# Two opening blocks' input prepared in chunks beside attention's last pair, with one tile that later blocks reuse

## Chip, cores and metric

The kernel runs on one core of a Trainium2 chip. The metric is the device time of one execution in microseconds (us), the median of several runs. The names of the engines are the profile's: PE is TensorE, PEld its weight load, DVE is VectorE, ACT is ScalarE, POOL is GpSimd, and SP is SyncE, whose queue issues most loads and stores.

## What is computed

Attention over 4 x 8 heads with 576 rows of 64 and rotated q and k, then two layers of two matrices each on its 2304 x 512 result. The reference, cut to what matters:

```python
q_rot, k_rot = rotate(q), rotate(k)
scores = scale * np.matmul(q_rot, k_rot.transpose(0, 1, 3, 2))
attn = softmax(scores)
x = np.matmul(attn, v)                      # 4 x 8 x 576 x 64, then 2304 x 512
h = np.maximum(x @ moe_w_in, 0.0)           # 2304 x 2048
x = h * h @ moe_w_out                       # 2304 x 512
h = x @ moe2_w_in
g = np.maximum(h, 0.0) + alpha * np.minimum(h, 0.0)
out = g @ moe2_w_out
```

The weights come as float64. Every product is made with operands split into a high and a low part, in three matmuls (high by high, high by low, low by high).

## The kernel before

*Attention* takes the heads in 16 pairs and each pair in 9 steps, 144 in all. A step makes scores on PE (L201), their maximum on DVE (L204), the exponential on ACT (L205), transposes on PE (L222, L234, L240, L241), which ACT copies to a high part (pth, ptth, L210) and DVE to a low part (ptl, pttl, L211), and the product with v (L267). POOL rotates k and q (L114 to L118) and splits v (vsplit, L127 and L128). The undivided result goes to x1 in DRAM (the names xd and x), the reciprocal sums (L250 to L258) to r1 (rd and r). SP moves the rotated operands to their places (kH, qT, kL, L169).

*The layers* (moe) work on 6 blocks of 384 columns. In layer 0 a block's x is made from three loads: two halves of x1, which are added (L502 or L533), and the reciprocals, by which the sum is multiplied (L503 or L534). ACT takes its high part xh (L509 or L538), DVE the low part xl (L514 or L543). For each of 16 input weights a unit of 12 matmuls makes ph (L552 to L554), ACT its relu g (L592), ACT or POOL its square; for each of 16 output weights a unit splits g into gh (ACT, L483) and gl (DVE, L484) and adds 12 matmuls to py (L570). The first two blocks run together, weight by weight (FIRST = 2): 32 units for the input weights, then 32 for the output weights. The later blocks use weights that lie ready. In layer 1 DVE makes mn (L595) and POOL adds it to g (L596).

*The weights* of layer 0 are converted while the opening blocks run: a load of 512 KB into one of four w64 buffers (L373), two operations on DVE (L382, L383), one more (L388), one on ACT (grow, L392), two on DVE (L397, L398), and the join on ACT (L403) and DVE (L404). The weights of layer 1 are converted beside the later blocks of layer 0, through one buffer (wc), stored to DRAM (wk, L454), and loaded again later (L460).

*What sets the order.* PE's order is written out everywhere. DVE's, ACT's and POOL's are written out from the layers' start on, and in attention a scheduler sets them. The layers' steps before their first unit run from attention's step 144 on (FOLLOW, follow): load_first, join_first, high_first and low_first for the two opening blocks, whole blocks of 4 chunks of 128x384 in two buffers (xr and r), and the first weights. Their space is what attention's pools ald (raw k, q, v), arope, acst, anat and akq leave, which close at step 143. The later blocks' x goes chunk by chunk (load_x, join_x, high_x, low_x) through one buffer of xr and r (pool xt1); each chunk's four steps are put at units by the job table:

```python
job((NF - 16 if before == (0, FIRST - 1) else at_unit[before + (1, 0)]) + 4 * c + 1,
    ((-2, load_x), (0, join_x), (1, high_x), (2, low_x)), layer, b, c)
```

Of the kernel before, what the change touches and what calls it, by code (L numbers as in the profile page):

```python
# [21 lines left out]
P = 128  # L22
# [14 lines left out]
FOLLOW = 0  # L37
# [4 lines left out]
def attention(tc, q, k, v, ident, ident_d, rope_d, xd, rd, follow):  # L42

# [8 lines left out]
    with ExitStack() as at:  # L52
# [30 lines left out]
        raw = {(x, nm): ld.tile([P, 4, 5, D], F32, name=f"{nm}raw{x}") for x in range(2) for nm in "kqv"}  # L83
# [223 lines left out]
        for s in range(len(steps) + LAG + OP + 3 * OPD + 8):  # L307
# [42 lines left out]
HELD0, OUT0, AHEAD = 4, 9, 2  # L350
XT0, CONV0, EVERY0, EVERY1, EVERY2 = 2, -8, 1.8, 1.8, 2.9
# [57 lines left out]
def moe(tc, xd, rd, mats, pbias, dram, al, out):  # L409
# [11 lines left out]
    with ExitStack() as mo:  # L421
        pool = lambda name, bufs, **kw: mo.enter_context(tc.tile_pool(name=name, bufs=bufs, **kw))
        st = pool("st", 1, side="right")
        held0 = pool("held0", HELD0, side="right")
        ps_h = pool("ps_h", 4, side="right", space=PSUM)
        xfirst = mo.enter_context(ExitStack())
        xtmp = mo.enter_context(ExitStack())
        xp = [xfirst.enter_context(tc.tile_pool(name="xp0", bufs=1, side="right"))]
        xp.append(xtmp.enter_context(tc.tile_pool(name="xt0", bufs=XT0, side="right")))
        mo.enter_context(tc.manual_schedule(engines={ET.PE, ET.DVE, ET.Activation, ET.Pool}))  # L430
# [56 lines left out]
        xin = {}  # L487

        def load_first(b):
            cs = slice(b * W, b * W + W)  # L490
            xr = xp[1].tile([P, KC, 2, W], F32, name="xr")
            r = xp[1].tile([P, KC, W], F32, name="r")
            for j in range(2):
                js = slice(64 * j, 64 * j + 64)
                for y in range(2):
                    nc.sync.dma_start(out=xr[js, :, y], in_=xd[j, 64 * y:64 * y + 64, :, cs])
                nc.sync.dma_start(out=r[js], in_=rd[:, j, cs].unsqueeze(0).to_broadcast([D, KC, W]))
            xin[b] = xr, r
# [232 lines left out]
```

## Time and profile before

| | |
|---|---|
| median of 3 runs | 1196.81 us (1196.57 to 1197.05) |
| profiled execution | 1196.49 us |
| its span in the profile | 1194.7 us |
| mean granted clock of PE | 0.978 of full speed |
| busy: PE, DVE, ACT, POOL | 1097.7, 694.4, 567.9, 378.7 us |
| attention's part | up to about 352 us |
| layer 0's part | about 352 to 760 us |

The sum is made against the profiled execution; the span is 1.8 us shorter than its time. Busy shares are means over the whole span, in which the stretches differ: PE is near full in most, and empty for some 17 us where attention ends.

### The profile page before, as it was taken

What the parts mean: (1) busy time and instruction counts of PE and PEld (TensorE: products, weight loads), DVE (VectorE), ACT (ScalarE), POOL (GpSimd) and SP (SyncE); (2) the same over time, 40 slices, a digit from 0 to 9 for tenths busy, and PEclk for the clock granted to TensorE, in tenths of its full rate; (3) what the DMA queues carried; (4) which work ended last, traced back from release to release, by engine and by line L of the source; (5) the groups of instructions that cost most, each with busy time, mean ns of one, the idle gap of its engine ahead of it and who ended that gap; (6) DMA issues with size and microseconds to landing.
All of it is one profiled execution on the core that took longest, in us unless ns stands there. A gap on an engine that the chain in (4) does not pass through costs nothing.

```text
span 1194.7 us, 17840 instructions
## 1 busy us (share of the span) xinstructions
PE 1097.7 (92%) x6480; PEld 1040.0 (87%) x6480; DVE 694.4 (58%) x1214; ACT 567.9 (48%) x1222; POOL 378.7 (32%) x351
## 2 busy tenths in 40 slices
PE   2899999999749979899999999999999999999998
PEld 1789889898639969799899999999898989899896
DVE  2788888888678887856767582223233332323332
ACT  1687887888625554445464553322223232323222
POOL 7956657650032220122122131113040413223140
PEclk9999999999969989999999999999999999999999
DMA  8867677555663442455757647860101001010101
GB/s 227 193 177 176 179 194 182 138 142 133 180 151 110 124 128 86 143 177 172 245 175 228 209 160 229 262 215 8 47 1 36 19 21 33 14 40 7 40 1 26
DMA packets 97174, 150.17 MB, mean 126 GB/s; under 512 B 21440, under 2 KB 66112, under 8 KB 97088
## 3 DMA queue, kind: packets, MB, share of 16 engines
q1 hardware_dynamic: 91472, 138.85, 41.5%
q10 hardware_dynamic: 5360, 10.07, 2.3%
q8 instruction: 51, 0.84, 0.3%
q14 instruction: 35, 0.29, 0.1%
q0 software_dynamic: 256, 0.13, 0.0%
HBM read 84.98 MB, written 35.73 MB: 101 GB/s over the span
## 4 chain that ended last, share of the span: by engine, by line
PE 60%; DVE 17%; DMA 7%; POOL 5%; ACT 5%; issue 3%; SPq 2%; ACTq 0%; POOLq 0%; DVEq 0%
PE py L570 21%; PE ph L553 9%; PE ph L554 9%; PE ph L552 9%; PE acc L267 4%; DMA xr<-x 3%; PE sc L201 3%; DVE w L397 3%; PE ps L222 2%; DVE m L383 2%; DVE w L404 2%; DMA kraw<-in_k_dram 2%; DVE w L398 1%; DVE nat L144 1%; DVE ptl L211 1%
## 5 line engine op out<-in xcount | busy, mean ns | idle before, releaser
L552 PE MATMUL ph<-xh,w 128*128 128x384 f32 x768 | 259.7, 338 | 9.1 <-ACT xh L538 5.5
L553 PE MATMUL ph<-xl,w 128*128 128x384 f32 x768 | 259.5, 338 | 2.7 <-DVE xl L514 2.2
L554 PE MATMUL ph<-xh,w 128*128 128x384 f32 x768 | 258.7, 337 | 0.0
L484 DVE TENSOR_TENSOR gl<-g,gh 128x384 fp32r<-128x384 f32 x192 | 109.0, 568 | 197.0 <-ACT gh L483 196.8
L596 POOL TENSOR_TENSOR g<-g,mn 128x384 f32<-128x384 f32 x96 | 101.8, 1060 | 295.6 <-DVE mn L595 295.6
L592 ACT ACTIVATE g<-ph 128x384 f32<-128x384 f32 x192 | 94.0, 489 | 202.0 <-PE ph L554 194.4
L570 PE MATMUL py<-w,gh 128*128 128x512 f32 x576 | 177.5, 389 | 0.0
L483 ACT ACTIVATE gh<-g 128x384 fp32r<-128x384 f32 x192 | 99.8, 522 | 154.1 <-PE py L570 130.7
L570 PE MATMUL py<-gh,w 128*128 128x384 f32 x640 | 167.8, 338 | 2.8 <-ACT gh L483 2.8
L552 PEld LDWEIGHTS ph<-xh,w 128*128 128x128 f32 x768 | 145.7, 190 | 12.9 <-ACT xh L538 6.4
L553 PEld LDWEIGHTS ph<-xl,w 128*128 128x128 f32 x768 | 145.6, 190 | 4.0 <-DVE xl L514 2.5
L554 PEld LDWEIGHTS ph<-xh,w 128*128 128x128 f32 x768 | 145.9, 190 | 0.0
L595 DVE TENSOR_SCALAR mn<-ph,al 128x384 f32<-128x384 f32 x96 | 59.3, 618 | 138.8 <-ACT g L592 132.1
L570 PEld LDWEIGHTS py<-w,gh 128*128 128x128 f32 x576 | 108.0, 188 | 22.2
L570 PEld LDWEIGHTS py<-gh,w 128*128 128x128 f32 x640 | 117.5, 190 | 3.5 <-ACT gh L483 3.5
L204 DVE TENSOR_REDUCE nm<-sc 128x1 f32<-128x576 f32 x144 | 105.9, 752 | 23.2 <-PE sc L201 21.6
L205 ACT ACTIVATE p<-sc,nm 128x576 f32<-128x576 f32 x144 | 106.4, 740 | 27.1 <-DVE nm L204 20.1
L570 PE MATMUL py<-w,gl 128*128 128x512 f32 x288 | 112.2, 389 | 0.0
L570 PE MATMUL py<-gl,w 128*128 128x384 f32 x320 | 108.5, 339 | 2.1 <-DVE gl L484 1.7
L211 DVE TENSOR_TENSOR ptl<-ps,pth 128x512 fp32r<-128x512 f32 (+1 forms) x160 | 99.9, 632 | 17.6 <-ACT pth L210 15.4
L600 POOL TENSOR_TENSOR g<-g 128x384 f32<-128x384 f32 x48 | 45.7, 953 | 188.1 <-ACT g L592 179.6
L210 ACT ACTIVATE pth<-ps 128x512 fp32r<-128x512 f32 (+1 forms) x160 | 86.9, 554 | 37.6 <-PE ps L222 36.5
(108 smaller groups left out, 1864.9 us busy)
## 6 DMA issues: line engine op xcount, KB each, us to landing
w<-in_moe_w_in_dram SPq DMA_DIRECT2D x32, 512.0 KB
w<-in_moe_w_out_dram SPq DMA_DIRECT2D x32, 512.0 KB
wk<-w SPq DMA_DIRECT2D x32, 512.0 KB
w<-wk SPq DMA_DIRECT2D x32, 512.0 KB
xr<-x SPq DMA_DIRECT2D x56, 192.0 KB
kH<-nat SPq DMA_DIRECT2D x64, 144.0 KB
qT<-nat SPq DMA_DIRECT2D x64, 144.0 KB
kL<-nat SPq DMA_DIRECT2D x64, 144.0 KB
```

What stands on the lines that cost most here:

```text
L204: V.tensor_reduce(out=nm, in_=sc[:, :, 0:SH], axis=AX.XY, op=ALU.max, negate=True)
L205: A.activation(out=Pt[n, i][:, j * S:(j + 1) * S].rearrange("p (a b) -> p a b", a=2), in_=sc[:, :, 0:SH], func=AF.Exp, bias=nm, accum_out= ...
L210: A.activation(out=sl(hi), in_=src, func=AF.Copy)
L211: V.tensor_tensor(out=sl(lo), in0=src, in1=sl(hi).bitcast(F32), op=ALU.subtract)
L483: A.activation(out=hi, in_=g, func=AF.Copy)
L484: V.tensor_tensor(out=lo, in0=g, in1=hi.bitcast(F32), op=ALU.subtract)
L552: T.matmul(ph[:, :W], lhsT=wh[:, cs], rhs=xh, start=(c == 0), stop=False)
L553: T.matmul(ph[:, :W], lhsT=wh[:, cs], rhs=xl, start=False, stop=False)
L554: T.matmul(ph[:, :W], lhsT=wl[:, cs], rhs=xh, start=False, stop=(c == KC - 1))
L570: T.matmul(acc, lhsT=x, rhs=y, start=(s0 and k == 0), stop=(s1 and k == 2))
L592: A.activation(out=g, in_=ph, func=AF.Relu)
L596: G.tensor_tensor(out=g, in0=g, in1=mn, op=ALU.add)
```

## The change

The opening blocks' x is loaded, joined and split chunk by chunk, by the same four functions as for the later blocks. The loads begin 14 steps before attention's end (AHEAD_X = 14, from step 130 on). For this attention's raw k, q, v, rotation and constants close at step 130 (front), except that their last v has a pool of its own (ald1); anat, akq and the scores' PSUM move to a second group (scored), which closes at step 143. The eight chunks follow each other every one and a half steps; the loads of weights 0 to 3 stand between them, while their conversion stays where it was.

The high and low parts of the opening blocks lie in one tile X (xs); later blocks reuse it in slices, and it also holds the conversion buffer of layer 1's weights (Xw[3]) and two output weights of layer 0 (Xw[4], Xw[5]). A second tile XT (xt) has two buffers for raw x and r, for all blocks, where later blocks had one; mn of layer 1 lies in it too. For the opening blocks both additions and the subtraction that makes the low part are on POOL.

```diff
-FOLLOW = 0
+AHEAD_X = 14
...
-        ld = fpool("ald", 1)
+        lds = [fpool("ald0", 1)]
+        cp = fpool("acst", 1)
         rp = fpool("arope", 1)
-        cp = fpool("acst", 1)
-        nat = fpool("anat", 1)
-        kq = fpool("akq", KQB)
-        front.enter_context(tc.manual_schedule(engines={mybir.EngineType.PE}))
-        ps_sc = fpool("ps_sc", NSC, space=PSUM)
+        lds.append(fpool("ald1", 1))
+        scored = at.enter_context(ExitStack())
+        nat = scored.enter_context(tc.tile_pool(name="anat", bufs=1))
+        kq = scored.enter_context(tc.tile_pool(name="akq", bufs=KQB))
+        scored.enter_context(tc.manual_schedule(engines={mybir.EngineType.PE}))
+        ps_sc = scored.enter_context(tc.tile_pool(name="ps_sc", bufs=NSC, side="right", space=PSUM))
...
+            if s == len(steps) - AHEAD_X:
+                front.close()
             if s == len(steps) - 1:
-                front.close()
-            if s >= len(steps) + FOLLOW:
+                scored.close()
+            if s >= len(steps) - AHEAD_X:
                 follow()
...
-HELD0, OUT0, AHEAD = 4, 9, 2
-XT0, CONV0, EVERY0, EVERY1, EVERY2 = 2, -8, 1.8, 1.8, 2.9
+HELD0, OUT0, OUTX, AHEAD = 4, 7, 2, 2
+CONV0, EVERY0, EVERY1, EVERY2 = -8, 1.8, 1.8, 2.9
...
+        X = pool("x", 1, side="right").tile([P, 2, KC, FIRST * W], F32R, name="xs")
+        Xf = X.rearrange("p y c w -> p (y c w)")
+        Xw = [Xf[:, 1024 * k:1024 * k + 1024].rearrange("p (y n) -> p y n", y=2) for k in range(6)]
+
+        XT = pool("xt", 1, side="right").tile([P, 2, 3, W], F32, name="xt")
         st = pool("st", 1, side="right")
...
         def slot(z, i):
+            if z and OUT0 <= i < OUT0 + OUTX:
+                return Xw[4 + i - OUT0]
...
-            return late["wc"].tile([P, 2, 512], F32R, name="w")
+            return Xw[3]
...
-        def load_first(b):
...
-        def join_first(b):
...
-        def high_first(b):
...
-        def low_first(b):
...
+        xin, xbuf = {}, itertools.cycle(range(2))
 
         def load_x(layer, b, c):
             c0 = b * W
-            xr = xp[1].tile([P, 2, W], F32, name="xr")
-            r = None
+            k = next(xbuf)
+            xr, r = XT[:, k, 0:2], XT[:, k, 2]
...
         def high_x(layer, b, c):
-            xh, xl = (xp[0].tile([P, W], F32R, name=nm) for nm in ("xh", "xl"))
+            if first(layer, b):
+                xh, xl = (X[:, y, c, b * W:b * W + W] for y in range(2))
+            else:
+                xh, xl = (Xf[:, (2 * c + y) * W:(2 * c + y) * W + W] for y in range(2))
...
         def low_x(layer, b, c):
             xh, xl = xsp[layer, b][c]
-            V.tensor_tensor(out=xl, in0=xin.pop((layer, b, c))[0][:, 0], in1=xh.bitcast(F32), op=ALU.subtract)
+            E = G if first(layer, b) else V
+            E.tensor_tensor(out=xl, in0=xin.pop((layer, b, c))[0][:, 0], in1=xh.bitcast(F32), op=ALU.subtract)
...
-                    mn = late["tp"].tile([P, W], F32, name="mn")
+                    mn = XT[:, u % 2, 2]
...
         for k in range(2 * FC):
...
+            if k < HELD0:
+                job(CONV0 + 2 * k, conv[0][1:], 0, 0, k)
+                continue
...
-        for b in range(FIRST):
-            for d, stage in ((-9, load_first), (b - 8, join_first), (2 * b - 7, high_first), (2 * b - 6, low_first)):
-                job(d, ((0, stage),), b)
...
+        for e in range(AHEAD_X):
+            for k in range(FIRST * KC):
+                for d, stage in ((0, load_x), (2, join_x), (2, high_x), (2, low_x)):
+                    if 3 * k // 2 + d == e:
+                        stage(0, *divmod(k, KC))
+            if e % 3 == 1 and e // 3 < HELD0:
+                weights.load(st, 0, 0, e // 3)
+            yield
+        late["held0"] = pool("held0", HELD0, side="right")
+        ps_h = pool("ps_h", 4, side="right", space=PSUM)
+        mo.enter_context(tc.manual_schedule(engines={ET.PE, ET.DVE, ET.Activation, ET.Pool}))
...
-            if t == at_unit[0, 0, 1, 0]:
-                xfirst.close()
-                xp[:] = pool("xp1", KC, side="right"), pool("xt1", 1, side="right")
-                late["wc"] = pool("wc", 1, side="right")
```

How this moves instructions: on POOL, behind the last vsplit (vs) of attention, before:

```order
L127 CAST vs<-vraw_111 128x10x64
L128 TENSOR_TENSOR vs<-vraw_111,vs 128x10x64
L503 TENSOR_TENSOR xr<-xr,r 128x4x384
L502 TENSOR_TENSOR xr<-xr 128x4x384
L503 TENSOR_TENSOR xr<-xr,r 128x4x384
L600 TENSOR_TENSOR g<-g 128x384 x16
```

and now (xt is the raw x, xs the high and low parts; three operations for each of eight chunks, of which the first is shown with what precedes it):

```order
L131 CAST vs<-vraw_114 128x10x64
L132 TENSOR_TENSOR vs<-vraw_114,vs 128x10x64
L512 TENSOR_TENSOR xt<-xt 128x384
L513 TENSOR_TENSOR xt<-xt 128x384
L526 TENSOR_TENSOR xs<-xt,xs 128x384
```

Three operations on whole blocks (and an add on DVE) became 24 on chunks, all of them still behind the last vsplit.

On ACT, around attention's last pth and ptth, before (w are operations of weight 0, xh is the first opening block's high part):

```order
L210 ACTIVATE pth<-ps 128x4x128
L210 ACTIVATE ptth<-ps 128x384
L210 ACTIVATE pth<-ps 128x4x128
L392 ACTIVATE w_4646<-w_4646,pbias 128x512
L509 ACTIVATE xh<-xr 128x4x384
L210 ACTIVATE pth<-ps 128x4x64 x2
L210 ACTIVATE ptth<-ps 128x128
L210 ACTIVATE ptth<-ps 64x64 x2
L255 ACTIVATE ri<-ps 9x128
```

and now:

```order
L214 ACTIVATE pth<-ps 128x4x128
L520 ACTIVATE xs<-xt 128x384
L214 ACTIVATE ptth<-ps 128x384
L214 ACTIVATE pth<-ps 128x4x128
L398 ACTIVATE w_4317<-w_4317,pbias 128x512
L520 ACTIVATE xs<-xt 128x384
L214 ACTIVATE pth<-ps 128x4x64 x2
L214 ACTIVATE ptth<-ps 128x128
L214 ACTIVATE ptth<-ps 64x64 x2
L520 ACTIVATE xs<-xt 128x384
```

The single xh ahead of the last pth became the fifth, sixth and seventh xs, and the seventh stands behind attention's ptth; the eighth follows later, ahead of the join of weight 0. The first xs stands further ahead, between two of the last pair's p:

```order
L209 ACTIVATE p,sums<-sc,nm 128x576
L520 ACTIVATE xs<-xt 128x384
L209 ACTIVATE p,sums<-sc,nm 128x576
L214 ACTIVATE pth<-ps 128x4x128
L214 ACTIVATE ptth<-ps 128x512
```

On SP, at block 3's x loads in layer 0 (wk is a store of a converted weight of layer 1, w the load of a raw one), before:

```order
L525 DMA r<-r_65 64x384 x2
L454 DMA wk_0_5_6672<-w 128x1024
L523 DMA xr<-x_64 64x2x384 x2
L373 DMA w_6797<-in_moe_w_in_dram 128x4x256
L454 DMA wk_0_6_6744<-w 128x1024
L525 DMA r<-r_65 64x384 x2
L373 DMA w_6864<-in_moe_w_in_dram 128x4x256
L523 DMA xr<-x_64 64x2x384 x2
L454 DMA wk_0_7_6818<-w 128x1024
L373 DMA w_6912<-in_moe_w_in_dram 128x4x256
L525 DMA r<-r_65 64x384 x2
L454 DMA wk_0_8_6885<-w 128x1024
```

and now:

```order
L504 DMA xt<-r_65 64x384 x4
L461 DMA wk_0_5_6676<-xs 128x1024
L502 DMA xt<-x_64 64x2x384 x2
L379 DMA w_6792<-in_moe_w_in_dram 128x4x256
L461 DMA wk_0_6_6743<-xs 128x1024
L379 DMA w_6856<-in_moe_w_in_dram 128x4x256
L504 DMA xt<-r_65 64x384 x2
L502 DMA xt<-x_64 64x2x384 x2
L461 DMA wk_0_7_6812<-xs 128x1024
L379 DMA w_6901<-in_moe_w_in_dram 128x4x256
```

The third chunk's x is loaded one weight earlier than before, the fourth two weights earlier, where the third's was.

## Rows read from the trace of the kernel before

**Rows 1.** Stretches: length, busy PE, PEld, DVE, ACT, POOL (instructions), PE's clock, DMA share, GB/s.

```profile
290.00:305.00 15.00, 15.00 (x123) 14.83 (x121) 13.09 (x25) 11.67 (x30) 2.08 (x2) 1.00 0.61 154
370.00:400.00 30.00, 29.86 (x172) 29.54 (x171) 25.41 (x42) 17.68 (x34) 6.29 (x6) 1.00 0.40 123
760.00:1195.00 435.00, 429.03 (x2208) 394.76 (x2206) 135.09 (x237) 121.05 (x244) 102.62 (x97) 1.00 0.15 45
```

**Rows 2.** PE's timeline, 317 to 446 us: start, duration, what [idle before <- releaser].

```profile
339.62 0.42 PE L240 MATMUL ps<-ident,p 128*64 128x128 f32 x1 [16.58 <-DVE pttl L211]
...
352.55 0.33 PE L552 MATMUL ph<-xh,w 128*128 128x384 f32 x1
...
358.05 0.61 PE L553 MATMUL ph<-xl,w 128*128 128x384 f32 x1 [2.22 <-DVE xl L514]
...
444.17 0.69 PE L570 MATMUL ph<-gl,w 128*128 128x384 f32 x1 [2.97 <-DVE gl L484]
```

**Rows 3.** The chain of waits, 318 to 357 us: start, duration, what.

```profile
320.25 10.32 DMA xr<-x
...
332.83 3.43 POOL xr L503
...
352.65 0.61 DVE w L397
...
353.75 0.69 DVE w L404
...
356.25 1.75 DVE xl L514
```

**Rows 4.** What waited for what, 515 to 760 us: us in total, times, longest.

```profile
PE ph L552 <- ACT xh L538: 5.5, 3, 2.3
```

**Rows 5.** Busy time by stretch, behind the first two of these waits.

```profile
586.00:592.00 6.00, 5.62 (x22) 5.36 (x23) 5.45 (x11) 4.59 (x9) 0.30 (x1) 0.72 0.54 177
657.00:663.00 6.00, 5.54 (x21) 5.28 (x22) 4.80 (x10) 3.84 (x8) 0.22 (x1) 0.72 0.60 216
```

**Rows 6.** SP's timeline: two x loads of block 3's chunks.

```profile
567.56 1.25 SPq L523 DMA_DIRECT2D xr<-x  x2
...
577.13 1.26 SPq L523 DMA_DIRECT2D xr<-x  x2
```

**Rows 7.** POOL's timeline: the last vsplit, and two adds of block 3.

```profile
303.64 1.54 POOL L128 TENSOR_TENSOR vs<-vraw,vs 128x640 fp32r<-128x640 f32 x1
...
572.21 1.03 POOL L533 TENSOR_TENSOR xr<-xr 128x384 f32<-128x384 f32 x1 [7.81 <-DMA xr<-x]
...
583.56 1.00 POOL L533 TENSOR_TENSOR xr<-xr 128x384 f32<-128x384 f32 x1 [9.17 <-DMA xr<-x]
```

**Rows 8.** POOL's line L533, 490 to 760 us: min/median/max in ns.

```profile
L533 POOL TENSOR_TENSOR xr<-xr x15: 996/1013/1358, 490.1 to 724.7; 128x384 f32<-128x384 f32 x15
```

**Rows 9.** ACT's timeline: attention's last pair, weights 0 and 1, block 3's last xh.

```profile
305.22 0.74 ACT L205 ACTIVATE p<-sc,nm 128x576 f32<-128x576 f32 x1
...
337.67 0.36 ACT L210 ACTIVATE pth<-ps 128x256 fp32r<-128x256 f32 x1
...
349.82 0.71 ACT L403 ACTIVATE w<-w 128x512 fp32r<-128x512 f32 x1 [0.47 <-DVE w L397]
350.44 0.77 ACT L392 ACTIVATE w<-w,pbias 128x512 uint32<-128x512 uint32 x1
...
585.66 0.52 ACT L538 ACTIVATE xh<-xr 128x384 fp32r<-128x384 f32 x1 [5.11 <-POOL xr L534]
```

**Rows 10.** DVE's line L543, 490 to 760 us.

```profile
L543 DVE TENSOR_TENSOR xl<-xr,xh x15: 548/552/559, 496.3 to 727.4; 128x384 fp32r<-128x384 f32 x15
```

**Rows 11.** DVE's line L211, 200 to 330 us.

```profile
L211 DVE TENSOR_TENSOR ptl<-ps,pth x69: 415/681/693, 199.8 to 321.5; 128x512 fp32r<-128x512 f32 x55, 128x256 fp32r<-128x256 f32 x14
```

**Rows 12.** DVE's timeline: one weight's L397 late in the opening.

```profile
428.82 0.69 DVE L397 SCALAR_TENSOR_TENSOR w<-w 128x512 uint32<-128x512 uint32 x1 [0.81 <-ACT w L392]
```

**Rows 13.** DVE's line L382, 330 to 450 us.

```profile
L382 DVE TENSOR_SCALAR m<-w x22: 417/420/3402, 333.1 to 447.2; 128x512 uint32<-128x512 uint32 x22
```

More of the change, by code (lines that the diff above doesn't have):

```diff
@@ L1 @@
+import itertools
 from contextlib import ExitStack
@@ L80, in attention @@
         rot = {}
-        raw = {(x, nm): ld.tile([P, 4, 5, D], F32, name=f"{nm}raw{x}") for x in range(2) for nm in "kqv"}
+        raw = {(x, nm): lds[(x, nm) == (1, "v")].tile([P, 4, 5, D], F32, name=f"{nm}raw{x}") for x in range(2) for nm in "kqv"}
         for x in range(2):
@@ L441, in slot @@
         def slot(z, i):
-            p = (held0 if i < HELD0 else late["held1"]) if z == 0 else late["out0" if i < OUT0 else "out1"]
-            return p.tile([P, 2, 512], F32R, name="w")
+            if z and OUT0 <= i < OUT0 + OUTX:
+                return Xw[4 + i - OUT0]
+            return late[("held0" if i < HELD0 else "held1") if z == 0 else ("out0" if i < OUT0 else "out1")].tile([P, 2, 512], F32R, name="w")
         def place(layer, z, i):
@@ L485, in split_g @@
             gsp[u] = hi, lo
-        xin = {}
-        def load_first(b):
[L490 to L498, printed above, removed]
-        def join_first(b):
-            xr, r = xin[b]
-            (G if b else V).tensor_tensor(out=xr[:, :, 0], in0=xr[:, :, 0], in1=xr[:, :, 1], op=ALU.add)
-            G.tensor_tensor(out=xr[:, :, 0], in0=xr[:, :, 0], in1=r, op=ALU.mult)
-        def high_first(b):
-            if b == 0:
-                xsp["first"] = [xp[0].tile([P, KC, XW], F32R, name=nm) for nm in ("xh", "xl")]
-            hi, lo = (t[:, :, b * W:b * W + W] for t in xsp["first"])
-            A.activation(out=hi, in_=xin[b][0][:, :, 0], func=AF.Copy)
-            xsp[0, b] = [(hi[:, c], lo[:, c]) for c in range(KC)]
-        def low_first(b):
-            hi, lo = (t[:, :, b * W:b * W + W] for t in xsp["first"])
-            V.tensor_tensor(out=lo, in0=xin.pop(b)[0][:, :, 0], in1=hi.bitcast(F32), op=ALU.subtract)
+        xin, xbuf = {}, itertools.cycle(range(2))
         def load_x(layer, b, c):
             c0 = b * W
-            xr = xp[1].tile([P, 2, W], F32, name="xr")
-            r = None
+            k = next(xbuf)
+            xr, r = XT[:, k, 0:2], XT[:, k, 2]
             if layer == 0:
-                r = xp[1].tile([P, W], F32, name="r")
                 for j in range(2):
@@ L627, in moe @@
         for k in range(2 * FC):
-            at = CONV0 + EVERY0 * k if k < HELD0 else EARLY + EVERY0 * (k - HELD0)
-            if k >= FC + OUT0:
-                at = max(at, at_unit[0, FIRST - 1, 1, FC // 2 - 1] - 2 + EVERY1 * (k - FC - OUT0))
+            if k < HELD0:
+                job(CONV0 + 2 * k, conv[0][1:], 0, 0, k)
+                continue
+            at = EARLY + EVERY0 * (k - HELD0)
+            if k >= FC + OUT0 + OUTX:
+                at = max(at, at_unit[0, FIRST - 1, 1, FC // 2 - 1] - 2 + EVERY1 * (k - FC - OUT0 - OUTX))
             job(at, conv[0], 0, k // FC, k % FC)
+        for k in range(2 * FC):
             job(NF + EVERY2 * k, conv[1], 1, k // FC, k % FC)
-        for b in range(FIRST):
-            for d, stage in ((-9, load_first), (b - 8, join_first), (2 * b - 7, high_first), (2 * b - 6, low_first)):
-                job(d, ((0, stage),), b)
         for c in range(KC):
@@ L645, in moe @@
             if t == EARLY:
-                xtmp.close()
-                late.update(held1=pool("held1", FC - HELD0), sp=pool("sp", 3), tp=pool("tp", 1), out0=pool("out0", OUT0),
+                late.update(held1=pool("held1", FC - HELD0), sp=pool("sp", 3), out0=pool("out0", OUT0),
                             g0=pool("g0", FC // 2), ps_y=pool("ps_y", 1, space=PSUM))
@@ L687, in fused_kernel @@
     rest = moe(tc, xd, rd, ((w_in1, w_out1), (w_in2, w_out2)), pbias, dram, al, out)
-    early = iter(range(STEPS_AHEAD + 1 + EARLY))
+    early = iter(range(AHEAD_X + STEPS_AHEAD + 1 + EARLY))
     def follow():
```

11 lines of the change are left out of this document (2 added, 9 removed).

## The prediction

> **What bounds the kernel now.** The first view is the busy time by stretch [rows 1]. From 290 to 305 us TensorE (PE) works 15.00 of 15.00 us and POOL only 2.08; from 370 to 400 PE works 29.86 of 30; from 760 on it works 429.03 of 435, and the list of waits has no wait of PE there. Where PE is full, nothing done on another engine can gain. The holes lie between.
>
> The second view, PE's timeline, names them [rows 2]. After attention's last full transposes PE waits 16.58 us, until 339.62, for attention's last pieces; its first matmul of the layers comes at 352.55; the second opening block waits 2.22 us for its xl; at 444.17 PE still waits 2.97 us for a gl that VectorE (DVE) makes.
>
> The third view, the chain of waits, tells what was late [rows 3]: the load of a whole block's x took 10.32 us, POOL's product with r 3.43. Behind them ScalarE (ACT) makes an xh, which stands in its order ahead of attention's last pth: attention's own end waits for the layers' x. Then the chain runs on DVE: weight 1, begun at 352.65 (behind ACT's part), is ready at 353.75 + 0.69 = 354.44, an xl of 1.75 us follows at 356.25, and so on to the wait at 444.17. DVE's stream of weights is the gate of the opening.
>
> Last, the later blocks: between 515 and 760 PE waits three times, 5.5 us in all, for the xh of a block's last chunk [rows 4], and after the first two of these the granted clock is 0.72 of full speed over 6 us [rows 5].
>
> **The change, part by part.** *The x loads.* Of 32 small loads one stands on SP ahead of the kH of attention's last pair; it shifts kH, qT and kL by one issue, 0.6 us (1.25 for two [rows 6]). PE is without a gap there [rows 1], so the shift is between nothing and 0.6 us; I take nothing, since everything behind it waits for x later on anyway.
>
> *The chunks.* Their 24 POOL operations stand behind the last vsplit in POOL's order, which ends at 303.64 + 1.54 = 305.18 [rows 7]. A 128x384 add or product takes 1.01 us by its median [rows 8]. The subtraction that makes xl is not in POOL's trace; L128's subtraction of 128x640 in 1.54 gives 0.93 by size, the add 1.01; I take 1.01. With ACT's 0.52 for an xh of this size [rows 9] and some 0.05 us for each of four handovers, a chunk takes 3 x 1.01 + 0.52 + 0.2 = 3.75 us from POOL's start to its xl. The buffer then goes to the chunk after next, whose load takes from its issue at 567.56 to POOL's start at 572.21, 4.65 us; the longest such, 577.13 to 583.56, is 6.43 [rows 6, 7]. Two buffers give a pace of (4.65 + 3.75) / 2 = 4.2 us a chunk. The first chunk ends at 305.18 + 3.75 = 309, the eighth at 309 + 7 x 4.2 = 338.4, plus the issues of the four weights which now stand among the x loads on SP (0.6 each, 2.4) and one lost handover of about 0.6 us between POOL and DVE: 341.4. Its xh, 1 us earlier, ends at 340.4.
>
> A rule of the Trainium skill would make this shorter: in "DMA: Bandwidth & Descriptors", section on the anatomy of one DMA, a transfer costs some 2.0 us plus its bytes at 436 GB/s, by estimate 3.4 us for a chunk's 0.59 MB. By it POOL's 3.75 us would set the pace, and the sum would come out 7 x 0.45 = 3.2 us lower, at 1172.8. The measured 4.65 decides, since such loads run beside other traffic.
>
> Another page of the Trainium skill, "GPSIMD Engine Reference", section on engine selection, speaks against the new place of xl: it gives elementwise work on two inputs to VectorE, where it is about twice as fast. The rows have 0.55 us for it on DVE against 1.01 [rows 8, 10]; by the rule the pace would be 0.23 us shorter and the sum 1.6 us lower if DVE had the time, which costs it 8 x 0.55 = 4.4 us.
>
> *Attention beside it.* The first xs stands in ACT's order between two p: it starts at 305.18 + 2.2 = 307.4, ends at 307.9, and the next p, at 305.22 before [rows 9], comes 2.7 us late. That delay has cover: attention's last pth stands behind the sixth xs (329 to 330), where it stood at 337.67 behind xh; if the cover were gone it would cost those 2.7 us. On DVE, L211 never took more than 0.69 us beside POOL's rope and vsplit [rows 11], so POOL's new work costs attention's DVE operations nothing.
>
> *The opening.* ACT joins weight 0 (0.71 us) and grows weight 1 (0.77) right behind the eighth xs [rows 9]: 340.4 + 1.5 = 341.9. DVE's three operations on it, which took from 352.65 to 354.44 [rows 3], make weight 1 ready at 343.7, where it was 354.44: 10.7 us earlier. One more xl (1.75) no longer stands ahead of weight 2, and DVE's usual wait of 0.81 us for ACT's grow comes back [rows 12]: 10.7 + 1.75 - 0.81 = **11.6 us** for all later weights. The waits of DVE behind POOL's 3.4 us operations (one L382 took 3.40 where 0.42 is the median [rows 13]) are inside these differences. PE itself could come earlier: first matmul at about 343, and then neither the 2.22 us nor the slow clock after it; so DVE's gate decides, and I take 11.6. Bounds: 14.8 by POOL's own pace; 7.1 with each POOL operation at its longest, 1.36 [rows 8], which makes a chunk 4.8 and the pace 4.7 (1.0 + 7 x 0.5 = 4.5 us later).
>
> *The later blocks.* With two buffers, chunk 3's x of block 3 is loaded where chunk 2's was, at 567.56 instead of 577.13. POOL then starts at 572 to 578, its xh comes not at 585.66 [rows 9] but some 5 us sooner, and PE, whose longest wait there is 2.3 us [rows 4], finds it there. The three waits go (5.5 us), and so does the slow clock behind two of them: 6 x 0.28 = 1.7 us each [rows 5], 3.4 us. Bounds: nothing and 8.9; I take **8.9**, since the new order has the earlier place.
>
> *The rest.* Layer 1's two mn buffers, the conversion buffer and two output weights inside X cost nothing: from 760 on PE waits for nobody [rows 1], and X is free once the opening's first half is done, long before these weights are converted.
>
> *Sum.* The profiled execution took 1196.49 us (span 1194.7); the median of the three runs is 0.3 above it. 1196.49 - 11.6 - 8.9 = **1176.0 us**.
>
> **The rivals.** (a) *The later waits stay*: the loads are earlier, but POOL and ACT keep their order, and xh stays behind something else. For it: several of these rows wait behind others in order. Against: POOL sat idle 9.17 us for this very DMA [rows 7]. Time: 1196.49 - 11.6 = 1184.9.
>
> (b) *The opening is given back*: POOL's operations at 1.36 and loads at 6.43 make (6.43 + 4.8) / 2 = 5.6 us a chunk, the eighth 1.0 + 7 x 1.4 = 10.8 us later, and only 0.8 us of the opening is left: 1196.49 - 0.8 - 8.9 = 1186.8. For it: DVE's weights and POOL's chunks meet from 333 on, and an L382 took 3.40 us behind POOL; the longest L533, 1.36, may show the other direction. The Trainium skill ("SBUF — State Buffer", section on who interferes with whom) states it as a lock: whichever of the two starts first keeps the other out until it ends.
>
> (c) *Slower*: each small load takes what the large one took, 10.32 us [rows 3], since weights are loaded beside it. The pace is (10.32 + 4.8) / 2 = 7.6, the eighth xs 1.0 + 7 x 3.4 = 24.8 us later than in my sum, and weight 0 and attention's end hang on it: 1196.49 + 24.8 - 20.5 = 1200.8. It decides from 20.5 / 7 = 2.9 us above my pace, 7.1 a chunk. Against: a chunk is an eighth of the bytes, and the large loads, of two blocks, were issued together.
>
> (d) *The change does not do what it says*: the loads wait for something of attention that ends late, and start only where the chain's old load did, at 320.25 [rows 3]. POOL's first chunk then starts at 320.25 + 4.65 = 324.9 instead of 305.18, 19.7 us later: 1196.49 + 19.7 - 20.5 = 1195.7. Against: the first load's place on SP is ahead of attention's last kH.
>
> **How the numbers follow.** My forecast has 0.64 (its own range 1171 to 1181, from 14.8 and 7.1 us for the opening, a little added below for the clock); (a) 0.12, (b) 0.10, (c) 0.04, (d) 0.04; 0.06 is left for a larger gain, if PE's clock stays up over the shorter gap. The range 1171 to 1188 takes in (a) and (b) and leaves (c), (d) and the larger gain out. About 0.2%, 2.4 us, is what can be told from no change. Faster 0.92 (forecast, (a), (b) and the larger gain); within it 0.04, which is (d); slower 0.04, which is (c).
>
> **What would show it.** Right: eight xs on ACT 4 to 5 us apart, the first near 307 and the last near 340; PE's L240 near 332, the first ph near 343; weight 1 ready near 344; no wait of PE for the xh of later blocks, and the clock at 1.00 there. Wrong: chunks over 5.6 us apart, weight 1 later than 350, or a wait of PE for xh at the later blocks of about the old size. Then the pace of the chunks, or the order on POOL, is the step that failed.

## The result, and the profile after

The changed kernel takes 1178.05 us (median of 4 runs, 1177.57 to 1178.72) where the kernel before, in the same comparison, takes 1196.93: a ratio of 0.9842, with a 95% interval from 0.9829 to 0.9856. That is 18.9 us or 1.6% faster; 1176.0 was forecast. The profiled execution took 1178.72 us (span 1176.9), 17.8 us less than that of before.

Where the time came from is seen best by one and the same operation in both traces. ACT makes a g after every unit of input weights (L592 before, L575 now), 192 in all, in the same order. The table compares the start of some of them; each difference is after minus before.

| g made by ACT, counted from 0 | before, us | after, us | difference |
|---|---|---|---|
| 0 (opening) | 363.46 | 354.01 | -9.45 |
| 24 (opening, near its end) | 419.09 | 409.66 | -9.43 |
| 36 (block 2) | 525.76 | 516.63 | -9.13 |
| 54 (block 3) | 601.52 | 588.62 | -12.90 |
| 72 (block 4) | 676.80 | 659.77 | -17.03 |
| 84 (block 5) | 737.02 | 718.77 | -18.25 |
| 186 (near the end) | 1146.04 | 1127.79 | -18.25 |

So the gain comes in two parts, as forecast, and nothing comes or goes in layer 1; the span is 17.8 us shorter and not 18.25, since the last store, issued 18.25 us earlier, takes 0.4 us longer. In between, among the output weights of the opening, the difference is smaller: the gh of ACT from the fifth on (436.37 now) come only 7.97 us earlier.

PE's timeline of the changed kernel, around attention's end and at the opening's output weights, answers to [rows 2]:

```profile
333.36 0.42 PE L244 MATMUL ps<-ident,p 128*64 128x128 f32 x1 [5.15 <-DVE pttl L215]
...
342.30 0.34 PE L535 MATMUL ph<-xs,w 128*128 128x384 f32 x1
...
354.56 0.69 PE L535 MATMUL ph<-xs,w 128*128 128x384 f32 x1 [3.76 <-ACT g L575]
```

```profile
421.33 0.44 PE L553 MATMUL py<-gh,w 128*128 128x384 f32 x1 [2.45 <-ACT gh L490]
423.32 0.69 PE L553 MATMUL py<-gl,w 128*128 128x384 f32 x1 [1.55 <-DVE gl L491]
...
436.20 0.69 PE L553 MATMUL ph<-gl,w 128*128 128x384 f32 x1 [3.99 <-DVE gl L491]
```

L244 (L240 before) waits 5.15 us instead of 16.58 and runs at 333.36, where 332 was forecast; the first ph is at 342.30 (343 forecast), and the second block's xl is never waited for. But the early start is lost again: PE has room for four units' ph, fills it, and waits 3.76 us for the first g, which ACT makes only behind its join of weight 3, at 354.01; the granted clock from 350 to 360 is 0.67. That is the forecast's own point, that DVE's stream of weights decides and not PE's first matmul. And the wait for a gl that was 2.97 us at 444.17 is now 3.99 at 436.20.

ACT's timeline answers to [rows 9]:

```profile
307.51 0.52 ACT L520 ACTIVATE xs<-xt 128x384 fp32r<-128x384 f32 x1 [1.94 <-POOL xt L513]
307.94 0.72 ACT L209 ACTIVATE p<-sc,nm 128x576 f32<-128x576 f32 x1
...
340.65 0.52 ACT L520 ACTIVATE xs<-xt 128x384 fp32r<-128x384 f32 x1
...
341.18 0.68 ACT L409 ACTIVATE w<-w 128x512 fp32r<-128x512 f32 x1
343.43 0.77 ACT L398 ACTIVATE w<-w,pbias 128x512 uint32<-128x512 uint32 x1 [1.57 <-DVE w L394]
```

The first xs stands where it was expected (307.51), and holds a p up to 307.94; the eighth comes at 340.65 (the forecast had it end at 340.4). The join of weight 0 is right behind. The grow of weight 1 is not: ACT sits idle 1.57 us for DVE's L394. DVE's timeline in the same place shows why:

```profile
336.92 0.89 DVE L254 TENSOR_SCALAR sums<-sums 128x9 f32<-128x9 f32 x1
...
337.98 1.31 DVE L403 SCALAR_TENSOR_TENSOR w<-w 128x512 uint32<-128x512 uint32 x1
339.32 1.13 DVE L404 TENSOR_SCALAR w<-w 128x512 uint32<-128x512 uint32 x1
...
341.55 1.38 DVE L389 SCALAR_TENSOR_TENSOR m<-w,m 128x512 f32<-128x512 uint32 x1
...
345.43 0.69 DVE L410 SCALAR_TENSOR_TENSOR w<-m,w 128x512 fp32r<-128x512 f32 x1
```

L254, L403, L404 and L389 take 0.89, 1.31, 1.13 and 1.38 us, where they take 0.41, 0.69, 0.43 and 0.69 by their medians: POOL's last chunk runs beside them. Weight 1 is ready at 345.43 + 0.69 = 346.12, not at 343.7.

At the later blocks PE has no wait for xs left from 500 to 745 us, and the windows that answer to [rows 5] have the full clock; blocks 3 and 4 begin in them. The last window is the opening's output weights, where the clock is 0.71 (it was 0.80 from 428 to 448 us before):

```profile
540.00:590.00 50.00, 49.38 (x283) 48.63 (x283) 40.55 (x69) 25.23 (x48) 13.32 (x12) 1.00 0.74 232
640.00:690.00 50.00, 50.00 (x290) 49.90 (x290) 35.44 (x62) 28.40 (x56) 12.87 (x12) 1.00 0.69 218
420.00:440.00 20.00, 13.13 (x49) 12.56 (x50) 18.08 (x28) 9.21 (x18) 6.80 (x6) 0.71 0.30 98
```

### The profile page after: what moved, and what is told of

Read it like the earlier page. It is cut to its first block, busy times and chain, and to the rows that moved or that the text cites. A ratio compares the mean times of both kernels' runs of the same rounds, so it can differ in the third digit from the quotient of the medians.

```text
span 1176.9 us, 17871 instructions
## 1 busy us (share of the span) xinstructions
PE 1097.0 (93%) x6480; PEld 1041.5 (88%) x6480; DVE 693.4 (59%) x1211; ACT 567.4 (48%) x1228; POOL 396.3 (34%) x372
## 4 chain that ended last, share of the span: by engine, by line
PE 68%; DVE 16%; ACT 4%; DMA 3%; issue 3%; POOL 3%; SPq 1%; ACTq 0%; POOLq 0%
PE py L553 24%; PE ph L535 9%; PE ph L536 9%; PE ph L537 9%; PE acc L271 5%; PE sc L205 5%; PE ps L226 3%; DVE w L403 3%; DVE m L389 2%; DVE w L404 2%; DVE m L388 2%; DVE gl L491 2%; PE ph L553 2%; DVE w L410 1%; DVE nat L148 1%
## 5 line engine op out<-in xcount | busy, mean ns | idle before, releaser
L535 PE MATMUL ph<-xs,w 128*128 128x384 f32 x768 | 258.6, 337 | 5.6 <-ACT g L575 5.6
L536 PE MATMUL ph<-xs,w 128*128 128x384 f32 x768 | 257.8, 336 | 0.0
L537 PE MATMUL ph<-xs,w 128*128 128x384 f32 x768 | 257.7, 336 | 0.0
L579 POOL TENSOR_TENSOR g<-g,xt 128x384 f32<-128x384 f32 x96 | 101.8, 1060 | 295.6 <-DVE xt L578 295.6
L575 ACT ACTIVATE g<-ph 128x384 f32<-128x384 f32 x192 | 93.7, 488 | 194.7 <-PE ph L537 187.2
L553 PE MATMUL py<-w,gh 128*128 128x512 f32 x504 | 155.3, 389 | 0.0
L535 PEld LDWEIGHTS ph<-xs,w 128*128 128x128 f32 x768 | 145.0, 189 | 7.6 <-ACT g L575 7.3
L553 PE MATMUL py<-gh,w 128*128 128x384 f32 x560 | 148.0, 339 | 2.8 <-ACT gh L490 2.8
L536 PEld LDWEIGHTS ph<-xs,w 128*128 128x128 f32 x768 | 145.0, 189 | 0.2
L537 PEld LDWEIGHTS ph<-xs,w 128*128 128x128 f32 x768 | 145.0, 189 | 0.0
L578 DVE TENSOR_SCALAR xt<-ph,al 128x384 f32<-128x384 f32 x96 | 59.3, 617 | 138.8 <-ACT g L575 131.7
L553 PEld LDWEIGHTS py<-w,gh 128*128 128x128 f32 x504 | 94.5, 188 | 19.4
L553 PEld LDWEIGHTS py<-gh,w 128*128 128x128 f32 x560 | 103.3, 191 | 3.5 <-ACT gh L490 3.5
L553 PE MATMUL py<-gl,w 128*128 128x384 f32 x280 | 95.8, 342 | 2.8 <-DVE gl L491 2.6
L553 PE MATMUL py<-w,gl 128*128 128x512 f32 x252 | 98.2, 390 | 0.0
```

What stands on the lines that cost most here:

```text
L535: T.matmul(ph[:, :W], lhsT=wh[:, cs], rhs=xh, start=(c == 0), stop=False)
L536: T.matmul(ph[:, :W], lhsT=wh[:, cs], rhs=xl, start=False, stop=False)
L537: T.matmul(ph[:, :W], lhsT=wl[:, cs], rhs=xh, start=False, stop=(c == KC - 1))
L553: T.matmul(acc, lhsT=x, rhs=y, start=(s0 and k == 0), stop=(s1 and k == 2))
L575: A.activation(out=g, in_=ph, func=AF.Relu)
L579: G.tensor_tensor(out=g, in0=g, in1=mn, op=ALU.add)
```

## The experiments

Every ratio is to the kernel before, in the same comparison; the changed kernel's own is 0.9842. A hundredth is 12 us. Since each run's ratio has an interval of some 0.0015 on either side, 2 us, the traces are compared too. Each trace carries an offset of its own: attention's last vsplit on POOL ends at 305.44 us in the changed kernel's, and up to 1.6 us earlier or later in those of the runs that leave attention alone, with the same distance from the first vsplit on. Where a reading below is of that size, the offset is given.

### Later blocks with one buffer

```diff
-            k = next(xbuf)
+            k = next(xbuf) if first(layer, b) else 0
```

> The changed kernel, but later blocks use only one of the two raw-x buffers (the opening keeps both). Theory (the second buffer alone took the waits at the later blocks): PE waits for the last chunk's xh of blocks 3, 4 and 5 again, 5.5 us, with the slow clock behind two of them, 3.4 us, and 0.9 us at block 2's start; POOL no longer joins block 2's second chunk beside the output weights, which gives 1.5 us back: about 1178 + 8.3 = 1186.3 us. Rival (the waits went because the opening moved everything else): 1178 us, and no wait of PE for xh.

Measured: 0.9894 (0.9877 to 0.9910), 6.2 us slower than the changed kernel. The waits come back, but smaller than in the kernel before (5.5 us), by the list of waits from 520 to 760 us:

```profile
PE ph L535 <- ACT xs L520: 3.2, 3, 1.6
```

The second buffer is what removes them. That they are 3.2 and not 5.5 us goes with the loads that they wait for: the last chunks of blocks 3, 4 and 5 took 4.65, 4.63 and 5.77 us from issue to POOL's start here, and 6.43, 5.99 and 5.60 before. The slow clock comes back only behind the third wait (1.58 us, then 0.72 over 6 us); behind the first two, 0.59 and 0.98 us, it stays at 1.00. In the g of ACT the three blocks lose 5.4 us on the changed kernel. The other side of the theory shows on POOL. First the changed kernel, then this run, POOL's timeline at the opening's output weights:

```profile
429.51 1.47 POOL L512 TENSOR_TENSOR xt<-xt 128x384 f32<-128x384 f32 x1
431.06 1.08 POOL L513 TENSOR_TENSOR xt<-xt 128x384 f32<-128x384 f32 x1
432.09 1.44 POOL L512 TENSOR_TENSOR xt<-xt 128x384 f32<-128x384 f32 x1
433.61 1.06 POOL L513 TENSOR_TENSOR xt<-xt 128x384 f32<-128x384 f32 x1
```

```profile
429.49 1.47 POOL L512 TENSOR_TENSOR xt<-xt 128x384 f32<-128x384 f32 x1
...
480.75 1.06 POOL L512 TENSOR_TENSOR xt<-xt 128x384 f32<-128x384 f32 x1 [48.65 <-DMA xt<-x]
```

With two buffers both chunks of block 2 that are loaded early are joined there, four operations in a row; with one the second waits until 480.75. DVE's timeline beside it, again first of the changed kernel, then of this run:

```profile
432.61 1.21 DVE L388 TENSOR_SCALAR m<-w 128x512 uint32<-128x512 uint32 x1
433.85 1.36 DVE L389 SCALAR_TENSOR_TENSOR m<-w,m 128x512 f32<-128x512 uint32 x1
```

```profile
432.57 0.41 DVE L388 TENSOR_SCALAR m<-w 128x512 uint32<-128x512 uint32 x1
433.02 0.69 DVE L389 SCALAR_TENSOR_TENSOR m<-w,m 128x512 f32<-128x512 uint32 x1
```

L388 and L389 take 1.21 and 1.36 us beside POOL's second join, 0.41 and 0.69 without it, and from there on the gh of ACT come 1.5 us earlier in this run than in the changed kernel. At block 2's start that is lost again: the g there are within 0.1 us of the changed kernel's, and PE waits 1.1 us for an output copy of ACT (L593), which the changed kernel has no wait for. So with the second buffer 1.5 us are lost in the opening and come back some 80 us later.

### The kernel before with two buffers

```diff
-                xp[:] = pool("xp1", KC, side="right"), pool("xt1", 1, side="right")
+                xp[:] = pool("xp1", KC, side="right"), pool("xt1", 2, side="right")
...
-                    mn = late["tp"].tile([P, W], F32, name="mn")
+                    mn = xp[1].tile([P, W], F32, name="r")
```

> The kernel before, with two raw-x buffers for the later blocks (mn of layer 1 lies in r's buffers, to make room), and the old opening. Theory (the two gains are separate): the three waits and the slow clock go, and the second chunk of block 2 is joined beside the output weights: 1196.9 - 8.3 = 1188.6 us, weight 1 ready at 354.4 as before. Rival (the second buffer helps only with the opening moved): 1196.9 us.

Measured: 0.9939 (0.9922 to 0.9956), 7.3 us faster than before; 8.3 was expected. In PE's timeline attention's end still waits for the large loads:

```profile
340.41 0.42 PE L240 MATMUL ps<-ident,p 128*64 128x128 f32 x1 [16.36 <-DVE pttl L211]
```

The waits for xh at later blocks are gone. From block 2 to block 5 the g of this run gain 10.0 us on the kernel before (from 1.5 us late to 8.5 early); of the 1.5 us 1.0 is there already at the last vsplit. The two halves of the change are thus separate, within the intervals: 12.7 us with the opening alone (the run above), 7.3 with the buffer alone, 18.9 together.

### Weight 1 begun earlier on DVE

```diff
-                job(CONV0 + 2 * k, conv[0][1:], 0, 0, k)
+                job(CONV0 + k, conv[0][1:], 0, 0, k)
```

> The changed kernel, with the conversion of weights 0 to 3 put at consecutive steps, so that DVE does weight 1's first three operations ahead of attention's last ones instead of behind weight 0's. Theory (weight 1 was late in the changed kernel because its grow waits for DVE's own first three operations on it, not for the eighth xs): weight 1 ready at about 345 instead of 346.1, weights 2 and 3 1.4 and 3.8 us earlier, and all behind them some 3.5 us earlier: 1174.5 us. Rival (the eighth xs, or attention's own end, sets the opening): weights 0 and 1 where they were, 1178 us.

Measured: 0.9820 (0.9805 to 0.9835), 2.6 us faster than the changed kernel, where 3.5 was expected; the intervals overlap, so the time alone doesn't decide. The trace shows the order at work. DVE's timeline, the last operation of weights 1 and 3 (345.43 and 353.90 in the changed kernel):

```profile
343.22 0.69 DVE L410 SCALAR_TENSOR_TENSOR w<-m,w 128x512 fp32r<-128x512 f32 x1
...
349.14 0.69 DVE L410 SCALAR_TENSOR_TENSOR w<-m,w 128x512 fp32r<-128x512 f32 x1
```

Weight 1 is 2.2 us earlier and weight 3 4.8. About 2 us of that are this execution's own: its last vsplit ends 1.55 us earlier, and its eighth xs came at 338.42 instead of 340.65. So weight 1 owes the order next to nothing, and weight 3 some 2.5 us; and PE's wait of 3.76 us for the first g is gone. The direction is the theory's; its size has these 2 us of doubt.

### All squares of the opening on ACT

```diff
-                elif i % 2 == 0:
+                elif i % 2 == 0 or first(layer, b):
```

> The changed kernel, with all squares of the two opening blocks on ACT (half of them were on POOL, 16 operations of 1 us). Theory (DVE's stream of weights is the gate, and POOL's operations on two inputs hold DVE's up): DVE's operations in the stretch of the input weights come back to 0.42 and 0.69 us, the cycle of a weight falls from 4.75 to about 4.3 us, and PE's wait between input and output weights shrinks: 3 to 6 us faster, 1172 to 1175 us. Rival (ACT, with 8.5 us more work, delays grow and join, or PE itself is the bound there): no gain or up to 4 us slower, 1178 to 1182 us.

Measured: 0.9761 (0.9745 to 0.9777), 9.7 us faster than the changed kernel, more than expected. The groups by line, 360 to 420 us (busy us, mean ns of one, then the idle time before them), first of the changed kernel, then of this run:

```profile
L583 POOL TENSOR_TENSOR g<-g 128x384 f32<-128x384 f32 x12 | 12.6, 1051 | 46.0 <-ACT g L575 46.0
...
L389 DVE SCALAR_TENSOR_TENSOR m<-w,m 128x512 f32<-128x512 uint32 x13 | 10.0, 770 | 0.4
...
L404 DVE TENSOR_SCALAR w<-w 128x512 uint32<-128x512 uint32 x13 | 8.6, 663 | 0.4
L388 DVE TENSOR_SCALAR m<-w 128x512 uint32<-128x512 uint32 x13 | 8.0, 614 | 0.0
```

```profile
L389 DVE SCALAR_TENSOR_TENSOR m<-w,m 128x512 f32<-128x512 uint32 x16 | 11.1, 693 | 0.6
...
L404 DVE TENSOR_SCALAR w<-w 128x512 uint32<-128x512 uint32 x15 | 6.4, 430 | 0.5
L388 DVE TENSOR_SCALAR m<-w 128x512 uint32<-128x512 uint32 x15 | 6.3, 421 | 0.0
```

Without the squares POOL has nothing in this stretch, and DVE's operations are back at 693, 430 and 421 ns; they had been 770, 663 and 614. That is half a microsecond a weight, and the cycle shows it: from weight 4 to weight 16 a weight takes 3.80 us (361.92 to 407.56) instead of 4.25 (359.96 to 410.98; the expectation's 4.75 was too long). It is not all: at the output weights, where PE waits for gl, the longest wait falls from 3.99 to 1.5 us and the clock stays at 1.00 from 420 to 440 instead of 0.71. Part of that last gain may be block 2's joins: with no squares ahead of them in POOL's order they ran as soon as their chunks were there. POOL's timeline, and the busy time by stretch (POOL's 0.00 is the last of the five engines):

```profile
344.96 1.02 POOL L512 TENSOR_TENSOR xt<-xt 128x384 f32<-128x384 f32 x1 [0.49 <-DMA xt<-x]
...
354.46 1.41 POOL L512 TENSOR_TENSOR xt<-xt 128x384 f32<-128x384 f32 x1 [4.27 <-DMA xt<-x]
```

```profile
420.00:440.00 20.00, 16.75 (x92) 15.48 (x91) 16.56 (x32) 10.20 (x19) 0.00 (x0) 1.00 0.35 105
```

That DVE's stream is the gate of the opening, and that POOL's operations hold it up, is shown by this run; how much of the 9.7 us is the squares' own and how much the joins' (1.5 us for one of them, in the run with one buffer later), it doesn't separate. By the Trainium skill ("SBUF — State Buffer", section on who interferes with whom) a DVE operation with two inputs in SBUF, or in a two-port mode, and a POOL operation that reads SBUF exclude each other for a whole operation; the rows at 429 to 435 us, shown with the run with one later buffer, agree, in which POOL's adds and DVE's L388 and L389 are both longer.

### Low parts on DVE

```diff
-            E = G if first(layer, b) else V
+            E = V
```

> The changed kernel, with the opening blocks' low parts made on DVE as in the kernel before, so that POOL has two operations a chunk instead of three. The page's rule (DVE is the better engine for it; the prediction's estimate): 1.6 us faster, 1176.4 us. Theory (the gate is DVE's stream, in order; an xl there waits for its xs with attention's ptl and the first weights behind it, but POOL holds DVE up less): between 1.5 us faster and 2 us slower, the eighth xs some 3 us earlier and weight 1 within 1 us of 346.1, about 1178 us. Rival (DVE's order stalls attention's end): over 1181 us.

Measured: 0.9855 (0.9840 to 0.9870), 1.6 us slower than the changed kernel, within the doubt of the two intervals, but not faster. DVE's line L526, 300 to 350 us, and the last xs in ACT's timeline:

```profile
L526 DVE TENSOR_TENSOR xs<-xt,xs x8: 547/558/1216, 309.2 to 344.2; 128x384 fp32r<-128x384 f32 x8
...
  ACT xs L520: 5.5, 5
```

```profile
343.66 0.53 ACT L520 ACTIVATE xs<-xt 128x384 fp32r<-128x384 f32 x1 [1.37 <-DMA r<-ri]
```

The operation is cheaper on DVE (558 ns against 1.0 us), but DVE sits idle 5.5 us in all for the xs, with attention's and the weights' operations behind it in order, and the eighth xs comes at 343.66 instead of 340.65, where 3 us earlier was expected. Of the 3.0 us 1.2 are this execution's own, by the last vsplit. What the prediction drew from the page "GPSIMD Engine Reference" of the Trainium skill, 1.6 us faster, is not seen here: the page compares one operation on two engines, and the place in the order decided.

### One buffer in the opening

```diff
-            k = next(xbuf)
+            k = 0 if first(layer, b) else next(xbuf)
```

> The changed kernel, with one raw-x buffer for the opening's chunks (later blocks keep two). Theory (a chunk's pace is half of load plus work with two buffers, and their sum with one): 4.65 + 3.75 = 8.4 us a chunk, the eighth xs near 366 instead of 340.7, weight 0's join right behind it, and some 25 us more than the changed kernel: 1203 us, slower than the kernel before. Rival (loads are quicker when only one chunk is under way, some 3 us): 6.8 us a chunk, the eighth xs near 355, 1192 us.

Measured: 0.9953 (0.9936 to 0.9969). This run doesn't answer the question: the program loads every second chunk ahead of the join of the one before it, so with one buffer the chunks of such a pair were joined from the wrong numbers, and no load waited for a join inside a pair. Between pairs the loads did wait (SP issues one at 305.05 us and the next at 315.97), other than the expectation of the second run has it. That run puts join and split ahead of the next load:

```diff
-            k = next(xbuf)
+            k = 0 if first(layer, b) else next(xbuf)
...
-                for d, stage in ((0, load_x), (2, join_x), (2, high_x), (2, low_x)):
+                for d, stage in ((0, load_x), (0, join_x), (0, high_x), (0, low_x)):
```

> The changed kernel, with one raw-x buffer for the opening's chunks and each chunk joined and split before the next is loaded (the earlier run with one buffer put the next load ahead of the join, so that most chunks were joined from other chunks' numbers and nothing waited for the join; its time says nothing of this). Theory (the pace of the chunks is load plus work, and behind some pace the eighth xs sets the opening): 4.65 + 3.75 = 8.4 us a chunk, the eighth xs near 366 instead of 340.7, weight 0's join right behind it: some 20 to 25 us more than the changed kernel, 1198 to 1203 us, no faster than the kernel before. Rival (DVE's stream of weights, or attention's end, hides most of it): under 1190 us.

Measured: 0.9973 (0.9963 to 0.9982), 15.7 us slower than the changed kernel, and still 0.3% faster than before. ACT's timeline, the first and the last xs, and PE's timeline, two of its waits:

```profile
309.10 0.52 ACT L520 ACTIVATE xs<-xt 128x384 fp32r<-128x384 f32 x1 [2.13 <-POOL xt L513]
...
367.99 0.52 ACT L520 ACTIVATE xs<-xt 128x384 fp32r<-128x384 f32 x1 [4.23 <-POOL xt L513]
```

```profile
360.52 0.69 PE L535 MATMUL ph<-xs,w 128*128 128x384 f32 x1 [5.84 <-ACT xs L520]
...
368.56 0.69 PE L535 MATMUL ph<-xs,w 128*128 128x384 f32 x1 [5.96 <-ACT xs L520]
```

The pace is (367.99 - 309.10) / 7 = 8.41 us a chunk, the sum of load and work, as the theory says; with two buffers it was (340.65 - 307.51) / 7 = 4.73. The eighth xs comes 27.3 us later, but only 17.7 us of it arrive in the g behind the opening. The reason is in PE's rows: block 0's four chunks are there at 336, its units begin at 346, and PE waits only for the last three of block 1's chunks, 3.61, 5.84 and 5.96 us; weights are converted in the meantime. The expectation held for the pace and was too high for the time.

### Begun 18 steps ahead

```diff
-AHEAD_X = 14
+AHEAD_X = 18
```

> The changed kernel, with the chunks begun 18 steps before attention's end instead of 14, so that two chunks stand ahead of the last vsplit in POOL's order and eight of their loads ahead of the last kH on SP. Theory (POOL's idle 16 us ahead of the last vsplit is usable, and the eighth xs and attention's end come earlier with the chunks): the first xs near 296, the eighth near 333, weight 1 ready 3 to 6 us earlier, 1172 to 1175 us. Rival (the space is free only when PE has read the last rotated operands, at 290, and eight issues of 0.65 us push kH, qT and kL by 5 us): PE waits 2 to 5 us in attention's last pair, vsplit comes later, and nothing is gained or up to 4 us lost, 1178 to 1182 us.

Measured: 0.9881 (0.9865 to 0.9898), 4.7 us slower than the changed kernel: the rival. The first xs does come at 296.29, but SP reaches the last kH only behind eight loads. SP's timeline, and PE's:

```profile
295.98 2.65 SPq L173 DMA_DIRECT2D kH<-nat  x4
```

```profile
302.08 0.50 PE L205 MATMUL sc<-kH,qT 128*128 128x288 f32 x2 [2.08 <-DMA qT<-nat]
305.97 0.82 PE L205 MATMUL sc<-kL,qT 128*128 128x288 f32 x2 [3.38 <-DMA kL<-nat]
```

kH is issued at 295.98 instead of 290.70, and PE waits 2.08 and 3.38 us for qT and kL. The eighth xs comes at 340.40, no sooner than before, since the later chunks fell behind by as much. In the change as it is, one load stands there, and PE has no such wait.

### Both edits that helped

```diff
-                job(CONV0 + 2 * k, conv[0][1:], 0, 0, k)
+                job(CONV0 + k, conv[0][1:], 0, 0, k)
...
-                elif i % 2 == 0:
+                elif i % 2 == 0 or first(layer, b):
```

> The changed kernel with both edits: weights 0 to 3 converted at consecutive steps, and all squares of the opening blocks on ACT. Theory (both shorten the same gate, DVE's stream, so they add until PE's own work is the bound): 4 us from the one and 9 from the other, less what PE then sets itself: 1164 to 1167 us. Rival (PE, full between the first units and the output weights, is already the bound with the squares moved): as with the squares alone, 1168 us.

Measured: 1166.19 us, 0.9739 (0.9723 to 0.9755), 12.3 us faster than the changed kernel and 31 faster than before. The two edits add, as the ratios have it (9.7 and 2.6 us alone): by the g of ACT this run is 4.1 us ahead of the one with the squares alone, of which 1.1 is there already at the last vsplit, and by the ratios 2.6. PE's busy time by stretch in the opening:

```profile
340.00:360.00 20.00, 19.76 (x116) 19.44 (x115) 19.02 (x29) 12.96 (x24) 6.44 (x5) 0.96 0.66 196
360.00:412.00 52.00, 51.54 (x297) 51.03 (x295) 42.35 (x79) 39.00 (x75) 0.00 (x0) 1.00 0.47 144
412.00:440.00 28.00, 21.53 (x114) 19.68 (x115) 23.42 (x46) 15.56 (x29) 0.00 (x0) 1.00 0.35 113
```

From 340 to 412 PE works 71.3 of 72 us. What is left is at the output weights, 21.53 of 28.

## Why the prediction was right, and where it was not

*The chunks.* Right in the sum. The first xs was expected at 307.4 and came at 307.51, the pace at 4.2 us plus some 3 us over all eight, and the eighth xs ends at 341.2 instead of 340.4. The steps are less even, 3.66 to 6.52 us from one xs to the next, and two terms were too small. The load was put at 4.65 us; where POOL waited for it in the opening it took 4.75, 4.90, 5.12 and 6.10 us. (The 4.65 are those of a later block's two x transfers alone, whose r transfers had been issued 3.1 us ahead of them.) And the third chunk's work took 5.41 us, not 3.75, since POOL waited 2.32 us for an xs that stood behind attention's pth and two p on ACT. Two rows show the load of the fifth chunk, SP's issue and POOL's start, 4.90 us apart:

```profile
319.32 0.60 SPq L502 DMA_DIRECT2D xt<-x  x1
```

```profile
324.22 1.00 POOL L512 TENSOR_TENSOR xt<-xt 128x384 f32<-128x384 f32 x1 [0.72 <-DMA xt<-x]
```

The figure that the prediction worked out from the page "DMA: Bandwidth & Descriptors" of the Trainium skill, 3.4 us, is shorter than each of these loads: the section gives it for one transfer on the gpsimd path, and a chunk's load here is four transfers, which SP issues 0.6 us apart.

*Attention beside it.* The delayed p (2.7 us both by forecast and trace) was covered: attention's last full transposes come 4.8 us later than before (325.73 instead of 320.92), and still L244 came at 333.36, 6.3 us earlier than L240 before. That the load ahead of kH costs nothing holds for one load; for eight it cost PE 5.5 us. That POOL's new work costs attention's DVE operations nothing does not hold in full: L254 took 0.89 us instead of 0.41.

*The opening* was forecast at 11.6 us and gave 9.45, and then 8.0 at the output weights: its sign and its gate were right, its size was not. The step that failed is that ACT joins weight 0 and grows weight 1 right behind the eighth xs. The join came there; the grow waited 1.57 us for DVE, whose operations on weights 0 and 1 were held up by POOL's last chunk, 0.6 to 0.7 us each in three of them, 2.0 in all. Without these 2.0 us L394 would, by estimate, have ended at 341.4, before ACT was free for the grow (341.86). Weight 1 came at 346.12 instead of 343.7: 1.6 us by this wait, 0.8 by the eighth xs itself. All later weights came some 9.4 us earlier than before, not 11.6.

The prediction had the row for such a hold-up, an L382 of 3.40 us behind POOL [rows 13]. In its sum it used it for what would vanish, and only rival (b) says that the new operations would meet DVE's too, without a price for DVE. What vanished is larger than that one row: in the kernel before an L382, attention's last L250 and the L397 of weight 0 took 3.40, 2.56 and 3.88 us beside POOL's three whole-block operations, where they take 0.42, 0.41 and 0.69 by their medians. Weight 0's join waited for the last of them, in DVE's timeline of before:

```profile
345.90 3.88 DVE L397 SCALAR_TENSOR_TENSOR w<-w 128x512 uint32<-128x512 uint32 x1
```

How the opening's gain divides between this and the earlier x, no run separates. The other 1.5 us, from 9.45 to 8.0, are the second chunk of block 2, which the second buffer brings beside the output weights; no step of the prediction had it, and they come back at block 2's start.

*The later blocks* were forecast at 8.9 us. From the output weights to block 5 they gave 18.25 - 7.97 = 10.3, of which 1.2 at block 2's start (that return, among others) and 9.1 at blocks 3 to 5: 3.8, 4.1 and 1.2. The waits and the slow clock behind two of them are gone, as forecast. Rival (a), that they stay, is out: they come back with one buffer. Not all of their size is the buffer's, though: with one buffer 3.2 us of waiting came back, not 5.5, with shorter loads, and the slow clock once, not twice.

*The other rivals.* (b) did not come: chunks were 4.73 us apart, not 5.6. (c) did not come either, and its bound, slower from 7.1 us a chunk, is refuted: at 8.41 us a chunk the kernel still was 0.3% faster than before. The error in (c) is that the eighth xs was taken as the start of all work, while PE and DVE go on with block 0. (d) did not come: the first load is issued at 289.99.

The sum came within about 2 us since an opening too large by 3.6 us met later blocks too small by 1.4; that it came so near is in part luck.

## What to carry to other kernels

When work moves to another engine, price it on the neighbour that it slows, not only on its own engine: here 1 us on POOL cost DVE 0.5 to 0.7 us where DVE was the gate, and taking 16 such operations off POOL gave 9.7 us, earlier joins on POOL included. A second buffer moves work earlier as well as removing waits, so look at what runs where it now lands. And loads put ahead in a queue delay whatever stands behind them there: eight of them put kH off by 5.3 us, and PE waited 5.5; one cost PE nothing.

## What was not expected of the hardware

The cost between POOL and DVE goes both ways and is about as long as what is left of the other's operation: beside each other at 429 to 435 us POOL's add takes 1.47 and 1.44 us instead of 1.01, and DVE's L388 and L389 1.21 and 1.36 instead of 0.42 and 0.69. DVE's operations on PSUM with one input in SBUF showed none of this [rows 11].

A wait can cost PE more than its length: in the changed kernel PE waits 2.45, 1.55 and 3.99 us between 418 and 437, the granted clock of 420 to 440 is 0.71, and 49 matmuls take 13.13 us of PE's time; with the squares on ACT the waits there are at most 1.5 us, the clock is 1.00, and 92 matmuls take 16.75. At that rate 49 would take 8.9 us, so by estimate some 4 us are the clock's. At the later blocks the clock of the 6 us behind a wait was 0.72 after waits of 2.32 and 1.90 us (kernel before) and 1.58 (one later buffer), and 1.00 after 1.26 (kernel before), 0.98 and 0.59 (one later buffer).
